# Retention then MLP: the first block's stores moved to ScalarE's queue, with a new order of loads and new planner numbers

## The chip, the cores and the metric

The kernel runs on one core of one Trainium2 chip. The metric is the time of one execution in device microseconds, lower is better. TensorE (PE in the profile) multiplies matrices, VectorE (DVE), ScalarE (ACT) and GpSimd (POOL) work on tiles, SyncE (SP) only issues DMAs here. 16 DMA engines move data for all of them.

## The reference, cut to what matters

```
B, H, S, D = 8, 8, 576, 64          # q, k, v: float32, B x H x S x D
scores = matmul(q, k^T) / sqrt(D)
gamma  = 1 - 2 ** (-5 - arange(H))
Dmat   = gamma[h] ** (i - j) if i >= j else 0
ret    = matmul(scores * Dmat, v)
x      = ret.transpose(0, 2, 1, 3).reshape(4608, 512)
h      = x @ w_in                   # 512 x 2048
g      = 0.5 * h * (1 + erf(h / sqrt(2)))
out    = g @ w_out                  # 2048 x 512, float32
```

## The kernel before

**Tiling.** The sequence of 576 is cut into four chunks of 128 and a tail of 64. A unit is one chunk of one batch (or the two tails of a pair of batches); 36 units of 128 tokens make nine blocks of 512 tokens. Units are taken in groups: groups 0 to 3 are the first chunks of the first four batches, one unit each (the "raw" units, in the tile `early`), and the groups from 4 on hold the same chunk of two batches. A group goes through these steps: its q and k are turned (groups 0 to 5 by TensorE, L454; the later ones by VectorE's 32x32 transposes, L548, with a copy that sorts them on ScalarE, L559), `scores` multiplies them into PSUM, `masked` multiplies by the mask on VectorE into `ret` (L612 for the raw units, L617 for the others), `inner` multiplies by v, `state` adds the chunk's keys times values to a running state, `cross` multiplies the state of the chunks before by q, and `evacuate` writes the result to the block's `x` tile.

**The two layers.** `mlp1` multiplies `x` by `w_in` and applies the Gelu on ScalarE (L816, L819) into `g_all`; `mlp2` multiplies by `w_out` into `o_sb`, which is stored. Block 0 is done in pieces of 128 or 256 tokens as its units and weights arrive. Later layers use a Strassen-like scheme with seven products in place of eight: `mlp2_fast` for the second half of block 0 and all later blocks, `mlp1_fast` for the last blocks. The products are named 1 to 7 and run in the order 1, 2, 6, 5, 7, 4, 3. They need sums of weights (`w_out_sums`, L870, eight instructions on VectorE, once all of `w_out` has landed) and of activations (`g_sum`, L883), intermediate copies `t` out of PSUM (`snap`, L485 on VectorE or L487 on ScalarE), and joins on VectorE into `o_sb` (L901). Product 7 of a half block needs the copy `t2` made after product 6.

**The order is written out by a planner.** The Python code that builds the kernel keeps planned times `T` for each engine and appends at each turn of the loop at L1303 what it thinks is ready next. On the chip nothing is reordered: each engine runs its own list in order and waits for semaphores. So a planner number (a landing, a duration, a threshold such as `LEAD`, `NEAR`, `AHEAD`, `JOIN`) acts only through the order that comes out. Where the planner sees a gap at the start it appends matmuls of zeros (`warm`, L1256).

**Loads.** All loads but those of unit 0 are issued by GpSimd (`load`, L305), in the order of the string `ORDER` (L376), then group by group (`reload`, L389). In it `wi5` is 256 columns of `w_in`, `wo2` 256 rows of `w_out`, `q7` the queries of unit 7, `n8` the keys of units 8 and 9 in a second layout, `io` and `dq2` computations of constants. `sw_dma` plans a landing: a time to issue, and a time to move in one queue.

**Stores.** `put` (L1247) appends the DMA of one finished `o_sb` to SyncE's list, or at the very end partly to ScalarE's. `STORE_AT` is the planner's earliest time for the stores of block 0; SyncE's list holds nothing but the first loads and the stores, so a store on it starts as soon as its `o_sb` is written. `share` is the planner's account of what a store takes from the loads. The pool of `o_sb` has four buffers (L114): q, k and v of unit 0 use the first three of them, block 0 writes four `o_sb`, and block 1's first `o_sb` comes into the buffer of block 0's first one.

Of the kernel before, what the change touches and what calls it, by code (L numbers as in the profile page):

```python
# [17 lines left out]
def kernel(  # L18
# [14 lines left out]
    nc = tc.nc  # L33
# [50 lines left out]
    N_XB = 4  # L84
    AHEAD = 35
    RATE = 0.4
    STORE_AT = 62.0
    CROWD = 66.0
    STATE10 = 28.0
    HOT = 8.0  # L90
    FETCH = 5.0
    ARRIVE = 5.4
    WARM_TO = 24.0
    JOIN = 1
    JOIN_SB = 0.0
    VISIT = 8
    LEAD = -3.0
    NEAR = 3.2
    SLACK, SB, PER_G, PER_B, TURN0 = 1.2, 2.0, 8.0, 20.0, 0.0
    FINE = 0.38  # L100
    FPOOL = 0.6
    N_V = 6
    N_WARM = 10
    MSK_AT = -58.0
    HK = N_DF // 2
# [16 lines left out]
    SEM = 0.12  # L122
    OVER = {"dve": 0.06}

# [97 lines left out]

    later = [(7.3, "act", 1.4, warm_gelu), (MSK_AT, "dve", 0.8, make_msk)]
    T["act"], T["dve"], T["pool"] = 2.6, 2.9, 1.25

# [15 lines left out]
    def sw_dma(issue, move):  # L241
        if len(flying) >= 8:
            T["pool"] = max(T["pool"], flying[-8])
        at = T["pool"]
        T["pool"] += issue
        sw[0] = max(sw[0] + move, at + ARRIVE + move - 0.9)
        flying.append(sw[0])
        return sw[0]
# [56 lines left out]
    def load(what, i):  # L305
# [3 lines left out]
        if what == "wi":  # L309
            nc.gpsimd.dma_start(w_in[:, :, i * 256:(i + 1) * 256],  # L310
                                moe_w_in[:, i * 256:(i + 1) * 256].rearrange("(c p) f -> p c f", p=128))
            land_in[i] = sw_dma(0.79, 1.35)
            return
# [10 lines left out]
        if what == "wo":  # L324
            nc.gpsimd.dma_start(w_out[:, 2 * i:2 * i + 2, :],
                                moe_w_out[i * 256:(i + 1) * 256, :].rearrange("(c p) f -> p c f", p=128))
            land_out[i] = sw_dma(0.75, 1.36) + 0.5
            return
# [4 lines left out]
        if what in "qk" and group_of[i] in BY_PE:  # L333
            dst = qk["qk".index(what)].rearrange("p (h e j d) -> p e h j d", h=HP, e=2, j=2)[:, :, :, j]
            for e in range(2):
                nc.gpsimd.dma_start(dst[:, e], {"q": q, "k": k}[what][2 * bp + j, HP * e:HP * e + HP, ci * C:ci * C + C, :].rearrange("h s d -> s h d"))  # L336
                land[what, i] = sw_dma(FPOOL, 0.48)
            return
# [12 lines left out]
        if what == "n":  # L351
            nc.gpsimd.dma_start(kn.rearrange("p j e h d -> p (j e h) d"),  # L352
                                k[2 * bp:2 * bp + 2, :, ci * C:ci * C + C, :].rearrange("b h s d -> s (b h) d"))
            land[what, i] = land[what, i + 1] = sw_dma(1.27, 1.8)
            return
        if what == "v" and i >= 4 and j is not None:
            nc.gpsimd.dma_start(v_ld.rearrange("p j h d -> p (j h) d"),  # L357
                                v[2 * bp:2 * bp + 2, :, ci * C:ci * C + C, :].rearrange("b h s d -> s (b h) d"))
            land[what, i] = land[what, i + 1] = sw_dma(1.27, 1.8)
            return  # L360
        src = {"q": q, "k": k, "v": v}[what]
        for jj in (j,) if j is not None else range(2):
            n = C if j is not None else TAIL
            if what == "v":
                dst = v_ld if i < 4 else v_ld[:, j] if j is not None else v_ld[n * jj:n * jj + n, 0]
            else:
                dst = qk["qk".index(what)] if i < 4 else qk["qk".index(what)][0:n, :, jj]
            nc.gpsimd.dma_start(dst, src[2 * bp + jj, :, ci * C:ci * C + n, :].rearrange("h s d -> s h d"))
            land[what, i] = sw_dma(0.88, 0.9) if j is not None else sw_dma(0.68, 0.5)

# [4 lines left out]
    cast_due["v", 0] = (loaded[0][1], first["first_v"])  # L375
    ORDER = ("wi4 io wo2 q2 q1 k1 k2 wi5 wi3 n4 v1 wi1 v2 wi0 wi2 k3 q3 v3 wi7 dq2 wi6 wo6 q4 wo4 q5 wo0 wo1 wo3 "  # L376
             "wo5 k5 wo7 q6 k4 k7 v4 q7 k6 q8 v6 q12 dq0 q9 v12 k9 k13 q10 n8 k11 k8 v8 dq3 k10 q11 v10 k12 n10 "
             "dq4 q13 n6 n12").split()

# [161 lines left out]
    def turn_dve(n, x):  # L541
# [6 lines left out]
        nc.vector.transpose(dst.rearrange("p (h b t) -> p h t b", h=HP, b=32), src)  # L548
        done = on("dve", 0.13 + m / 530, max(land["qk"[x], i] for i in groups[n])) + SEM
        if x == 0:  # L550
# [4 lines left out]
    def apart():  # L555
# [4 lines left out]
                       sg[n]["pairs"].rearrange("p h s -> p (h s)")[:, 0:2 * m].rearrange("p (n y) -> p y n", y=2))  # L560
        sg[n]["T"] = max(sg[n].get("T", 0.0), on("act", 0.15 + m / 580, ready) + SEM)

# [241 lines left out]
    def act_dur(n):  # L804
        return 0.12 + n * 0.00084

# [440 lines left out]
    def put():  # L1247
        ready, t, ts, o_sb, lo, hi = stores.pop(0)
        rows = rows_of(t, ts)
        for m, (row, p0, n) in enumerate(rows):  # L1250
            ending = t == N_BLK - 1 and all(x[-1] == "3" for x in waiting2 if x[1] == t)
            queue = nc.scalar if ending and (m if len(rows) > 1 else ts % 2 == 0) else nc.sync
            queue.dma_start(out[row:row + n, lo:hi], o_sb[p0:p0 + n, lo:hi])
        share(T["pe"], 0.75 * (hi - lo) / d_model)

# [193 lines left out]
```

## Time and profile before

| | us |
|---|---|
| median of 3 runs | 287.59 (287.58 to 287.60) |
| the profiled execution | 288.46 |
| its span | 286.7 |
| TensorE busy in the span | 277.8 (97%) |
| VectorE, ScalarE, GpSimd busy | 229.7, 176.7, 141.0 |
| matmuls of zeros | 24 |
| last product's end, then join, store and its landing | from 282.95 to the end of the span |

The span lies 1.8 us below the profiled execution's own time, and the profiled execution 0.9 us above the median of the runs. Times within the span are counted from its start. In the timeline rows the first column is the start, the second the time from the start to the end of the merged group, and what stands in brackets is the engine's idle time before it and who ended it. "DMA to landing" counts from the start of the issuing instruction.

### The profile page before, as it was taken

Reading aid. Unit: us, or ns where it says so; the run is one execution under the profiler, and the core shown is the slowest. Engines: PE = TensorE matmul, PEld = TensorE weight load, DVE = VectorE, ACT = ScalarE, POOL = GpSimd, SP = SyncE. Lnnn points to the kernel's source line nnn. Section 1 sums busy time; section 2 is a strip of 40 time slices with the busy share of each in tenths; the row PEclk is TensorE's granted clock in tenths of the full one; section 3 lists DMA queues with packets and bytes.
Section 4 is the critical chain, followed back from the end, with each engine's and each line's share of the span. In section 5 each row is a group of like instructions: output and inputs, shape, how many; then the busy total and the mean of one; then the engine's idle time right before and its main releaser. Section 6 shows DMA issues by size and latency. Waiting matters only on the chain.

```text
span 286.7 us, 9851 instructions
## 1 busy us (share of the span) xinstructions
PE 277.8 (97%) x4216; PEld 210.3 (73%) x4216; DVE 229.7 (80%) x387; ACT 176.7 (62%) x403; POOL 141.0 (49%) x213
## 2 busy tenths in 40 slices
PE   7889998999999999999999999999999999999994
PEld 2568766888864657756676676677888888888883
DVE  6754586767995699898978599969999999999861
ACT  7456425876888895688587766764555363655421
POOL 8976898799959977778665864000000000000000
PEclk9999999999999999999999999999999999999999
DMA  9999999999999999999999996302020201202014
GB/s 158 176 179 188 195 152 173 188 132 143 128 154 108 116 167 120 205 146 135 142 150 160 101 139 54 71 2 75 2 75 0 77 4 72 75 0 75 37 57 129
DMA packets 109276, 31.97 MB, mean 112 GB/s; under 512 B 85936, under 2 KB 104880, under 8 KB 109232
## 3 DMA queue, kind: packets, MB, share of 16 engines
q0 software_dynamic: 100528, 21.12, 83.8%
q1 hardware_dynamic: 6752, 9.37, 9.9%
q10 hardware_dynamic: 1952, 0.85, 1.3%
q8 instruction: 33, 0.54, 0.8%
q14 instruction: 11, 0.09, 0.1%
HBM read 42.99 MB, written 9.44 MB: 183 GB/s over the span
## 4 chain that ended last, share of the span: by engine, by line
PE 61%; DMA 22%; POOL 12%; issue 2%; ACT 1%; DVE 0%; POOLq 0%
PE psum L450 60%; DMA kn_ld<-in_k_dram 6%; DMA w_out<-in_moe_w_out_dram 6%; DMA q_ld<-in_q_dram 5%; POOL k_ld L346 3%; POOL q_ld L346 2%; DMA v_ld<-in_v_dram 2%; DMA early<-in_q_dram 2%; POOL v_ld L357 2%; DMA k_ld<-in_k_dram 1%; POOL dqT L320 1%; PE psum L454 1%; POOL kn_ld L352 1%; POOL w_in L310 1%; POOL k_ld L336 1%
## 5 line engine op out<-in xcount | busy, mean ns | idle before, releaser
L450 PE MATMUL psum<-x,w_in 128*128 128x256 bf16 (+2 forms) x792 | 117.8, 295 | 0.6 <-DMA w_in<-in_moe_w_in_dram 0.6
L450 PEld LDWEIGHTS <-w_in 128*128 128x128 bf16 x792 | 69.0, 98 | 29.1 <-DMA w_in<-in_moe_w_in_dram 1.2
L450 PEld LDWEIGHTS <-g_all 128*128 128x128 bf16 x576 | 55.5, 98 | 13.5 <-issue 0.3
L450 PE MATMUL psum<-w_out,g_all 128*128 128x256 bf16 (+1 forms) x440 | 57.9, 280 | 0.0
L346 POOL DMA_DIRECT2D k_ld<-in_k_dram x64 | 35.5, 577 | 23.8 <-DMA kn_ld<-in_k_dram 14.1
L816 ACT ACTIVATE g_all<-psum 128x512 bf16<-128x512 f32 x64 | 36.9, 592 | 16.4 <-PE psum L450 14.8
L450 PEld LDWEIGHTS <-s 128*128 128x128 bf16 x408 | 39.5, 98 | 7.6 <-issue 0.6
L634 ACT ACTIVATE vh<-v_ld,dv 128x128 bf16<-128x128 bf16 (+1 forms) x144 | 42.1, 378 | 0.0
L617 DVE TENSOR_TENSOR ret<-psum,msk 128x1024 bf16<-128x1024 f32 (+1 forms) x32 | 35.5, 1149 | 6.3 <-PE psum L450 6.2
L1030 ACT ACTIVATE g_all<-t 128x512 bf16<-128x512 f32 x36 | 22.6, 630 | 28.2 <-DVE t L1038 28.2
L487 ACT COPY t<-psum 128x256 f32<-128x256 f32 (+1 forms) x48 | 20.7, 433 | 29.7 <-PE psum L450 29.5
L346 POOL DMA_DIRECT2D q_ld<-in_q_dram x64 | 35.6, 583 | 1.9 <-DMA k_ld<-in_k_dram 1.0
L450 PE MATMUL psum<-wt,s 128*128 128x256 bf16 x272 | 33.5, 273 | 0.3 <-ACT t L487 0.3
L901 DVE TENSOR_TENSOR o_sb<-psum,t 128x256 f32<-128x256 f32 x51 | 21.4, 420 | 13.1 <-PE psum L450 7.2
L1038 DVE TENSOR_TENSOR t<-psum,t 128x512 f32<-128x512 f32 x36 | 24.6, 687 | 2.7 <-ACT t L487 1.1
L819 ACT ACTIVATE g_all<-psum 128x256 bf16<-128x256 f32 (+1 forms) x43 | 19.5, 488 | 11.2 <-PE psum L450 10.6
L485 DVE COPY t<-psum 128x512 f32<-128x512 f32 (+1 forms) x39 | 21.6, 564 | 0.4 <-PE psum L450 0.3
L450 PE MATMUL psum<-x,ws 128*128 128x256 bf16 x144 | 19.5, 273 | 0.0
L450 PE MATMUL psum<-wt,g_all 128*128 128x256 bf16 x136 | 17.5, 273 | 0.0
L450 PE MATMUL psum<-w_out,s 128*128 128x256 bf16 x136 | 17.5, 273 | 0.0
L357 POOL DMA_DIRECT2D v_ld<-in_v_dram x14 | 16.5, 1180 | 1.0 <-ACT g_all L816 0.7
L785 DVE TENSOR_TENSOR x<-psum,dqT 128x1024 bf16<-128x1024 f32 (+1 forms) x14 | 15.5, 1137 | 0.1
(100 smaller groups left out, 326.2 us busy)
## 6 DMA issues: line engine op xcount, KB each, us to landing
out_dram<-o_sb SPq DMA_DIRECT2D x31, 256.0 KB, 3.3
q_ld<-in_q_dram POOLq DMA_DIRECT2D x56, 64.0 KB, 5.5
k_ld<-in_k_dram POOLq DMA_DIRECT2D x56, 64.0 KB, 4.7
v_ld<-in_v_dram POOLq DMA_DIRECT2D x14, 256.0 KB, 5.3
kn_ld<-in_k_dram POOLq DMA_DIRECT2D x12, 256.0 KB, 6.8
w_in<-in_moe_w_in_dram POOLq DMA_DIRECT2D x8, 256.0 KB, 8.4
w_out<-in_moe_w_out_dram POOLq DMA_DIRECT2D x8, 256.0 KB, 7.1
q_ld<-in_q_dram POOLq DMA_DIRECT2D x16, 32.0 KB, 4.5
```

The source lines that it names most:

```text
L346: nc.gpsimd.dma_start(qk["qk".index(what)][p0:p0 + 32, 0:HP * per].rearrange("p (h x) -> p h x", h=HP), {"q": q, "k": k}[what][2 * bp + jj ...
L357: nc.gpsimd.dma_start(v_ld.rearrange("p j h d -> p (j h) d"), v[2 * bp:2 * bp + 2, :, ci * C:ci * C + C, :].rearrange("b h s d -> s (b h) d"))
L450: nc.tensor.matmul(*a, **k)
L485: nc.vector.tensor_copy(dst, src)
L487: nc.scalar.copy(dst, src)
L617: nc.vector.tensor_tensor(both.rearrange("p (e h) s -> p e h s", e=2), t, by, op=ALU.mult)
L634: nc.scalar.activation(vh[:, 0:m, h], src[:, :, h], AF.Copy, scale=dv[:, h, ci:ci + 1])
L816: nc.scalar.activation(g_all[:, t % 2, :, m0, :], hT.rearrange("p n (a c) -> p (n a) c", a=2), AF.Gelu)
L819: nc.scalar.activation(g_of(t, 2 * lo // TOK)[:, m0:m0 + n, lo_:lo_ + hi - lo], hT, AF.Gelu)
L901: nc.vector.tensor_tensor(dst, src, f[key], op=ALU.add)
L1030: nc.scalar.activation(g_of(t, part)[:, m0:m0 + 2], src, AF.Gelu)
L1038: nc.vector.tensor_tensor(f[key], f["b"][1], f[key], op=ALU.add)
```

## The change: what it does

The planner's numbers are changed, and `put`. Three things come out of it in the instruction lists. (1) The four stores of block 0 (256 KB each) leave SyncE's list and stand on ScalarE's, one behind the other, between the twelfth and the thirteenth Gelu of block 1. (2) GpSimd's list of loads has the same transfers in another order. (3) TensorE's list holds the same matmuls in another order, with 29 of zeros in place of 24; the attention steps come in the same number of visits (14 of scores for the full groups, five joint ones of two groups from `inner` on), except that the scores of the last two tails stand together. VectorE's mask instructions L213 and L215 move behind the first L612. Some copies out of PSUM change between VectorE and ScalarE, and four joint L785 become eight L789. The order of the last products is the same.

```diff
-    AHEAD = 35
-    RATE = 0.4
+    AHEAD = 18
+    RATE = 5.8
     STORE_AT = 62.0
-    CROWD = 66.0
-    STATE10 = 28.0
+    CROWD = 200.0
+    STATE10 = 12.0
...
-    JOIN = 1
+    JOIN = 0
     JOIN_SB = 0.0
     VISIT = 8
-    LEAD = -3.0
-    NEAR = 3.2
+    LEAD = -2.0
+    NEAR = 1.6
...
-    FINE = 0.38
-    FPOOL = 0.6
+    FINE = 0.35
+    FPOOL = 0.55
...
-    MSK_AT = -58.0
+    MSK_AT = 18.0
...
-    OVER = {"dve": 0.06}
+    OVER = {"dve": 0.08, "act": 0.09}
...
-    T["act"], T["dve"], T["pool"] = 2.6, 2.9, 1.25
+    T["act"], T["dve"], T["pool"] = 2.6, 2.9, 1.4
...
-        sw[0] = max(sw[0] + move, at + ARRIVE + move - 0.9)
+        sw[0] = max(sw[0] + move, at + (ARRIVE if at < 4.0 else 3.9) + move - 0.9)
...
-            land_in[i] = sw_dma(0.79, 1.35)
+            land_in[i] = sw_dma(0.78, 1.32)
...
-            land_out[i] = sw_dma(0.75, 1.36) + 0.5
+            land_out[i] = sw_dma(0.75, 1.28) + 0.3
...
-                land[what, i] = sw_dma(FPOOL, 0.48)
+                land[what, i] = sw_dma(0.74, 0.44)
...
-            land[what, i] = land[what, i + 1] = sw_dma(1.27, 1.8)
+            land[what, i] = land[what, i + 1] = sw_dma(1.17, 1.68)
...
-            land[what, i] = sw_dma(0.88, 0.9) if j is not None else sw_dma(0.68, 0.5)
+            land[what, i] = sw_dma(0.88, 0.9) if j is not None else sw_dma(0.7, 0.55)
...
-    ORDER = ("wi4 io wo2 q2 q1 k1 k2 wi5 wi3 n4 v1 wi1 v2 wi0 wi2 k3 q3 v3 wi7 dq2 wi6 wo6 q4 wo4 q5 wo0 wo1 wo3 "
-             "wo5 k5 wo7 q6 k4 k7 v4 q7 k6 q8 v6 q12 dq0 q9 v12 k9 k13 q10 n8 k11 k8 v8 dq3 k10 q11 v10 k12 n10 "
-             "dq4 q13 n6 n12").split()
+    ORDER = ("wi1 io wi7 k1 n4 v2 wi5 q1 q2 k2 wi0 dq2 v1 q3 wi4 v3 wi2 k3 wo2 wo7 wi6 k4 wi3 wo1 wo0 wo3 wo5 k5 "
+             "wo4 wo6 k6 q4 q5 v4 q8 v8 n8 q6 k9 q7 k7 v6 q10 n6 k8 q9 k11 k10 v12 q11 k13 v10 n10 dq3 n12 q12 k12 "
+             "dq0 q13 dq4").split()
...
-        done = on("dve", 0.13 + m / 530, max(land["qk"[x], i] for i in groups[n])) + SEM
+        done = on("dve", m / 457 - 0.02, max(land["qk"[x], i] for i in groups[n])) + SEM
...
-        sg[n]["T"] = max(sg[n].get("T", 0.0), on("act", 0.15 + m / 580, ready) + SEM)
+        sg[n]["T"] = max(sg[n].get("T", 0.0), on("act", 0.18 + m / 595, ready) + SEM)
...
-        return 0.12 + n * 0.00084
+        return 0.16 + n * 0.00084
...
-            queue = nc.scalar if ending and (m if len(rows) > 1 else ts % 2 == 0) else nc.sync
+            queue = nc.scalar if t == 0 or ending and (m if len(rows) > 1 else ts % 2 == 0) else nc.sync
+            if t == 0:
+                on("act", 0.6)
             queue.dma_start(out[row:row + n, lo:hi], o_sb[p0:p0 + n, lo:hi])
-        share(T["pe"], 0.75 * (hi - lo) / d_model)
+        share(T["pe"], 1.2 * (hi - lo) / d_model)
```

More of the change, by code (lines that the diff above doesn't have):

```diff
@@ L358, in load @@
                                 v[2 * bp:2 * bp + 2, :, ci * C:ci * C + C, :].rearrange("b h s d -> s (b h) d"))
-            land[what, i] = land[what, i + 1] = sw_dma(1.27, 1.8)
+            land[what, i] = land[what, i + 1] = sw_dma(1.17, 1.68)
             return
```

## The prediction

> **What bounds the kernel now.** I read the page first, then the busy times by stage, the waits of TensorE, the chain that ended last, and the timeline of each engine around the waits.
>
> ```profile
> span 286.7 us, 9851 instructions
> PE 277.8 (97%) x4216; PEld 210.3 (73%) x4216; DVE 229.7 (80%) x387; ACT 176.7 (62%) x403; POOL 141.0 (49%) x213
> PE   7889998999999999999999999999999999999994
> DMA  9999999999999999999999996302020201202014
> q0 software_dynamic: 100528, 21.12, 83.8%
> ```
> ```profile
> 9.00:16.00 7.00, 6.12 (x97) 3.95 (x97) 5.57 (x12) 1.88 (x5) 6.04 (x9) 1.00 1.92 177
> 16.00:33.00 17.00, 16.10 (x315) 14.43 (x311) 7.06 (x12) 10.44 (x26) 13.02 (x18) 1.00 1.67 187
> 33.00:41.00 8.00, 7.99 (x45) 3.95 (x43) 7.02 (x12) 1.61 (x4) 6.50 (x9) 1.00 1.73 156
> 41.00:51.03 10.03, 8.90 (x203) 7.19 (x201) 6.88 (x9) 5.18 (x14) 8.99 (x14) 1.00 1.60 167
> 51.03:283.00 231.97, 231.53 (x3537) 177.90 (x3536) 196.39 (x312) 150.69 (x343) 98.56 (x153) 1.00 0.82 98
> ```
>
> TensorE is busy for 97% at a granted clock of 1.00, and the same matmuls run after the change. So the time can move only by TensorE's idle time and by matmuls of zeros, which count as busy. In the 232 us after 51.03 it idles 0.44 us: there is next to nothing to win, and only something to lose. Before that it idles 0.88, 0.90 and 1.13 us in three stages, beside the zeros. The DMA digits stay at 9 until some 170 us: the loads' queue q0 is full, and at the start it sets what TensorE can do.
>
> ```profile
> PE psum L454 <- DMA q_ld<-in_q_dram: 1.1, 1, 1.1
> PE psum L450 <- DMA w_in<-in_moe_w_in_dram: 0.6, 1, 0.6
> PE psum L450 <- ACT t L487: 0.3, 1, 0.3
> 45.94 0.61 PE L454 MATMUL psum<-ident,q_ld 128*128 128x128 bf16 x8 [1.08 <-DMA q_ld<-in_q_dram]
> 39.69 6.11 DMA q_ld<-in_q_dram
> ```
> ```profile
> L1253 SPq DMA_DIRECT2D out_dram<-o_sb x2: 356/358/361, 40.5 to 41.0; - x2
> DMA to landing us min/median/max: 5.2/5.4/5.7
> L1253 SPq DMA_DIRECT2D out_dram<-o_sb x2: 332/332/332, 50.7 to 51.6; - x2
> DMA to landing us min/median/max: 5.7/6.0/6.3
> ```
>
> The longest wait after the first microseconds is for the queries of group 5. Their last DMA is issued at 39.7 and lands at 45.8, and in between SyncE starts the first two stores of block 0, at 40.5 and 41.0, because nothing holds its queue back. The other two start at 50.7 and 51.6.
>
> **Stores: what goes.** The first pair no longer collides with group 5's queries, so the 1.08 us at 45.94 goes, if nothing else is late at that place. What is late next there is the queue itself, in the new order. I rebuild it from four landings on the chain that ended last, each row's start plus its time.
>
> ```profile
> 4.14 6.38 DMA early<-in_q_dram
> 18.43 9.51 DMA w_out<-in_moe_w_out_dram
> 28.94 7.12 DMA w_out<-in_moe_w_out_dram
> ```
>
> That is q1 at 10.5, wo6 at 27.9 and wo5 at 36.1. Between the last two the queue landed five pieces of w_out and four of 64 KB in 8.1 us: 1.28 each and 0.43 each. Between the first two it landed eight weights and seven 128 KB transfers in 17.4 us; with 1.30 and 0.88 that is 16.6, so 0.8 us was lost underway.
>
> **Loads: the new order up to 51 us.** At 10.5 the new order has landed the same amount (wi1, wi7, k1, v2). From there wi5 comes at 11.8, q1 at 12.7, q2 at 13.6, k2 at 14.5, wi0 at 15.8, v1 at 16.7, q3 at 17.5, and k3 at 21.9, or 22.7 with the 0.8 lost. From k3 to the last w_out are ten weights and two pairs of 64 KB (14.5 us): 36.4 to 37.2. Then k6, q4 and q5, three pairs, end at 39.0 to 39.8.
>
> ```profile
> 7.58 1.47 PE L450 MATMUL psum<-zeros 128*128 128x512 bf16 x6
> 9.67 0.40 PE L450 MATMUL psum<-ret,early 128*32 128x128 bf16 x14 [0.36 <-DVE ret L612]
> 7.11 0.47 DVE L213 TENSOR_SCALAR msk<-val 128x128 f32<-128x128 f32 x1
> 8.32 1.29 DVE L612 TENSOR_TENSOR ret<-psum,near 128x512 bf16<-128x512 f32 x2
> 14.09 0.81 PE L450 MATMUL psum<-zeros 128*128 128x512 bf16 x3
> 28.98 2.41 PE L450 MATMUL psum<-x,w_in 128*128 128x128 bf16 x40
> 31.23 0.61 PE L454 MATMUL psum<-ident,q_ld 128*128 128x128 bf16 x8
> 33.01 8.12 PE L450 MATMUL psum<-w_out,g_all 128*128 128x512 bf16 x40
> 51.03 0.62 PE L450 MATMUL psum<-q_ld,kT 32*128 32x128 bf16 x32
> 51.59 3.67 PE L450 MATMUL psum<-x,w_in 128*128 128x256 bf16 x32
> 55.18 0.63 PE L450 MATMUL psum<-ret,vh 128*32 128x128 bf16 x32
> 56.35 7.16 PE L450 MATMUL psum<-x,w_in 128*128 128x256 bf16 x64
> ```
>
> Before, the masks from 7.11 to 8.32 stand ahead of the first L612; behind it, they let unit 0's second half start some 0.5 us sooner, at 9.1 where the zeros end. TensorE then has four zeros (0.22 each by the row at 14.09) and reaches its first w_in at 10.3. From there to 17.5 it follows the landings above, and the five zeros more (1.1 us) lie in these gaps: they cost nothing of their own, and if the loads came earlier they would cost up to 1.1. It turns q3 at 17.6 to 17.8. The work from there to k3's turn (inner of unit 2, a state, 64 matmuls with w_in) is 4.4 us at the paces of the rows (0.056 for 128 columns: 40 from 28.98 to 31.23), so TensorE is there at 22.2 and waits 0 to 0.5. The rest of block 0's first layer is 10.1 us more: it ends between 32.6 and 33.1. Before it ended at 33.01, with a turn of 0.44 (31.23 to 31.67) in it that now comes later: 32.6 for the same work. So the start is 0 to 0.5 us slower; I take 0.3, nearer to the later end, since 0.8 us was lost in the same stretch of the queue before.
>
> From 33.01 to 51.03 it was 18.0 us. Without the idle 1.08, and with the turn of 0.44 that has moved in, it is 17.4, so the point that stood at 51.03 comes at 50.0 to 50.5. The turn of group 4's queries is due 6.9 to 7.0 after the first layer's end, at 39.5 to 40.1, and finds them landed at 39.0 to 39.8: hardly any cover, so 0.5 us of delay in the queue costs up to 0.5. Group 5's queries come after three 256 KB loads (as four of 64 KB, 1.7 each) and four pairs, 8.5 us behind q5: 47.5 to 48.3, and they are due at 48 to 48.5. That cover is as thin. The eight L870 start when the last w_out lands, as before, and end ahead of the first scores. This part is worth 0.5 to 1.0 us; I take 0.7.
>
> **Stores: what comes.** ScalarE now issues them after the twelfth Gelu of block 1.
>
> ```profile
> L1253 ACTq DMA_DIRECT2D out_dram<-o_sb x4: 499/556/600, 281.3 to 283.4; - x4
> 53.45 1.56 ACT L819 ACTIVATE g_all<-psum 128x512 bf16<-128x512 f32 x3
> 51.10 2.44 ACT L634 ACTIVATE vh<-v_ld,dv 128x128 bf16<-128x128 bf16 x8
> 43.92 2.35 DVE L617 TENSOR_TENSOR ret<-psum,msk 128x1024 bf16<-128x1024 f32 x2 [0.96 <-PE psum L450]
> 42.54 0.42 DVE L901 TENSOR_TENSOR o_sb<-psum,t 128x256 f32<-128x256 f32 x1 [0.24 <-PE psum L450]
> 72.57 0.69 DVE L883 TENSOR_TENSOR s<-g_all 128x1024 bf16<-128x1024 bf16 x1
> ```
>
> Four issues of 0.56 are 2.2 us of ScalarE. Queued behind them are the last four Gelus of block 1, a cast of the state and the copies `t` of product 1; TensorE waits for these only when its PSUM banks run out. ScalarE is busy for 150.7 of 232 us in this stage, and its list there (cast, eight scaled values of 2.4, a sorting copy, Gelus of 0.5) puts the first issue at 64 to 65.5. I cost the issue itself at 0 for that slack, at most 0.5.
>
> The landing is the dearer part. From 50.3 on, TensorE's list has twice 48 matmuls with w_in (0.11 each), a scores visit (0.56) and an attention visit (1.2, 55.18 to 56.35), 64.5; then 24, scores to 67.8, 8 and the products 1 and 2: 70.5. The join of product 2, L901, writes into the buffer of block 0's first store. With a store's 5.2 to 6.3 us this buffer is free at 70 to 71.5. Behind the waiting L901 on VectorE stand an L883 (0.69) and the copy `t2` (as long as the join, 0.42), on which product 7 waits. Masks (2.35 after the scores at 67.8), join, sum and copy end at about 72.1, and product 7 is due at 72.3, two products after product 2. So a late landing passes to TensorE in full. I take 0, the ends are 0 and 1.
>
> **The rest.** The late loads have slack: their bytes and their order by groups are unchanged from group 9 on, and TensorE's only wait on another engine after 51.03 is the 0.3 for a copy `t`. I count 0.1 gained there, with bounds of -0.4 and +0.5, since the new lists put other work ahead of each copy. The four L785 split in two add some 0.1 each on VectorE, beside TensorE's work. The last products and joins are the same list: nothing.
>
> The sum is 0.7 + 0.1 = 0.8 us off the span, 285.9, and with the 1.8 us around it 287.7 for a profiled execution. That of before (288.46) lies 0.87 above the median of the runs, so 286.8.
>
> **A page on shared engines.** The Trainium skill, "DMA: Bandwidth & Descriptors", section "Issuing engines are not separate DMA queues", says that DMAs started by ScalarE, SyncE or GpSimd end up on the same 16 engines and interleave. The 6.11 us of group 5's queries beside SyncE's stores agree with it. By this page moving a store to another queue saves nothing by itself; only its new time can.
>
> **The rivals.** *The new place collides too, and VectorE pays* (slower). Four stores in a row at 65 on a full queue, 1 MB where pairs were sent before: if the first lands over 5.5 us after its issue, or is issued past 65.5, L901 waits, then the copy, then product 7. With twice the pair's traffic, 8 us to landing, the wait is some 2.3 us, 289.1, and a third of it gives 287.6. For it: the chain above has 0.2 us of slack. Against: the first store of a pair had 5.2 and 5.7, and the others stand behind it. I put it at 288.5, with 0.25.
>
> *The start eats the gain* (no change). The queue holds TensorE from 10 to 23 us; with the 0.8 us lost ahead of q3 instead of behind it, or with group 4's queries late by 0.5, the 0.7 us is gone: 287.6. The 29 zeros speak for it. 0.14.
>
> *The collision is only moved* (no change). The stores push the loads behind them by some 2.4 us (group 5's queries, a weight, a 256 KB load and five pairs after 36.1, would have landed at 43.4, not 45.8), and if a later group's turn then waits 1 us, as group 5's did, it is 287.6. Against it: the second pair at 50.7 pushed them too, and no wait on a DMA came after 51. 0.06.
>
> *All small waits go* (faster). The late 0.44 goes too, and the start does not lose its 0.3: 286.8 - 0.4 - 0.3 = 286.1. The landings at their earlier values speak for it, VectorE's 196 busy us of 232 after 51.03 against it. 0.12.
>
> **How the numbers follow.** About 0.2%, 0.58 us, is what can be told from no change. My forecast of 286.8 has 0.43; most of it (0.39) lies below 287.0. Faster: 0.39 + 0.12 = 0.51. Same: 0.04 + 0.14 + 0.05 = 0.23. Slower: 0.25 + 0.01 = 0.26. The range runs from 285.8, just past the faster rival, to 288.5, the middle of the slow one.
>
> **What would show it.** Right: no wait of TensorE on q_ld near 46, the first scores of group 5 0.5 to 1 us nearer to the start for the same work, four stores on ScalarE's queue at 64 to 65.5 with 5 to 6 us to landing, and less than 0.5 us of idle TensorE after that. Wrong: L901 near 70 idle on a DMA of o_sb and TensorE idle before product 7; a wait on early or q_ld at 17 to 23 or at 40; or new waits on `t` copies late in the span.

## The result, and the profile after

| | before | after |
|---|---|---|
| median of the runs, us | 287.60 (287.53 to 288.66, 6 runs) | 295.86 (295.27 to 296.40, 6 runs) |
| ratio | 1 | 1.028 [1.026, 1.030] |
| profiled execution, its span | 288.46, 286.7 | 296.32, 294.5 |

The change costs 2.8%, and the spans of the two profiled executions differ by 7.8 us. The page after:

```profile
span 294.5 us, 9865 instructions
PE 280.8 (95%) x4221; PEld 211.0 (72%) x4221; DVE 227.3 (77%) x386; ACT 179.0 (61%) x408; POOL 140.7 (48%) x213
PE   7889999999999999599999899999999999999995
DMA  9999999999999999999999991302010202100214
q0 software_dynamic: 100528, 21.12, 81.6%
```

TensorE is no longer full in the middle: one slice shows 5. The busy times by stage (length, then PE, PEld, DVE, ACT, POOL, then PEclk) say where, and the waits of TensorE behind 30 us say for whom:

```profile
51.28:64.50 13.22, 13.22 (x263) 11.05 (x264) 10.39 (x11) 11.35 (x28) 12.80 (x20) 1.00 1.66 143
73.90:119.00 45.10, 45.10 (x938) 29.80 (x936) 38.73 (x58) 34.27 (x87) 35.95 (x57) 1.00 1.22 123
119.00:129.00 10.00, 6.60 (x61) 3.72 (x60) 5.22 (x9) 6.07 (x15) 6.69 (x11) 0.83 1.55 155
155.00:167.00 12.00, 10.85 (x131) 7.06 (x130) 9.41 (x12) 9.68 (x25) 9.36 (x16) 1.00 1.62 145
124.80:128.20 3.40, 3.40 (x34) 1.84 (x34) 1.45 (x2) 1.92 (x5) 3.36 (x5) 0.50 1.05 85
```
```profile
PE psum L450 <- ACT u_acc L709: 3.4, 1, 3.4
PE psum L450 <- DVE t L485: 1.1, 1, 1.1
PE psum L450 <- DVE ret L617: 0.7, 2, 0.4
PE psum L454 <- DMA k_ld<-in_k_dram: 0.3, 1, 0.3
```

The wait on `q_ld` at 46 is gone. In its place TensorE idles 3.4 us before 123.6, then runs 3.4 us at a granted clock of 0.50, which by an estimate costs another 1.7 (half of the 3.4). Here are TensorE and then ScalarE at that place:

```profile
118.30 1.90 PE L450 MATMUL psum<-x,w_in 128*128 128x512 bf16 x8
123.60 1.03 PE L450 MATMUL psum<-w_out,g_all 128*128 128x256 bf16 x8 [3.40 <-ACT u_acc L709]
```
```profile
116.08 0.60 ACT L816 ACTIVATE g_all<-psum 128x512 bf16<-128x512 f32 x1
120.64 2.44 ACT L634 ACTIVATE vh<-v_ld,dv 128x128 bf16<-128x128 bf16 x8 [3.96 <-DMA v_ld<-in_v_dram]
122.99 1.04 ACT L709 COPY u_acc<-psum 128x512 f32<-128x512 f32 x2
```

The eight scaled values (`vh`) of group 14 stand on ScalarE's list ahead of the copies of the state (L709), and nothing overtakes them. Their load lands at 120.6. Until then PSUM is not emptied and TensorE stops. Before, the same L634 stood behind L709 and began 7 us after its load had landed (at 118.6 by the trace's DMA records, which hold the time of each landing). So the landing is 2.0 us later than before, and the place in the list is about 9 us earlier: ScalarE comes to it at 116.7. ScalarE of the kernel before:

```profile
120.63 1.18 ACT L709 COPY u_acc<-psum 128x512 f32<-128x512 f32 x2 [1.49 <-DVE u_sb L707]
125.51 2.43 ACT L634 ACTIVATE vh<-v_ld,dv 128x128 bf16<-128x128 bf16 x8
```

A smaller case of the same kind is on VectorE, before TensorE's wait of 1.14 us at 166.40. A turn (L548) that waits for group 19's queries stands ahead of the copies `t`:

```profile
161.51 1.10 DVE L548 STREAM_TRANSPOSE qT<-q_ld 128x512 f32<-128x512 f32 x1 [2.06 <-DMA q_ld<-in_q_dram]
165.05 1.05 DVE L548 STREAM_TRANSPOSE kT<-k_ld 128x512 f32<-128x512 f32 x1
165.96 0.39 DVE L485 COPY t<-psum 128x256 f32<-128x256 f32 x1
```

The start, which was forecast to end (first `w_out` product) at 32.6 to 33.1:

```profile
12.12 0.62 PE L450 MATMUL psum<-x,w_in 128*128 128x128 bf16 x8 [0.76 <-DMA w_in<-in_moe_w_in_dram]
20.03 3.26 PE L450 MATMUL psum<-x,w_in 128*128 128x256 bf16 x40 [0.75 <-DMA w_in<-in_moe_w_in_dram]
29.13 5.03 PE L450 MATMUL psum<-x,w_in 128*128 128x128 bf16 x72 [0.50 <-ACT x L487]
34.00 1.24 PE L450 MATMUL psum<-w_out,g_all 128*128 128x512 bf16 x5
```

And block 0's stores (the four of L1255 on ScalarE's queue between 60 and 75 us):

```profile
L1255 ACTq DMA_DIRECT2D out_dram<-o_sb x4: 367/669/1120, 64.6 to 66.4; - x4
DMA to landing us min/median/max: 6.3/6.7/7.0
```

**A ledger of the runs.** A sum of idle times can't be compared between lists of another order. So every matmul but those of zeros gets the mean spacing of its kind in the trace of before (from its start to the next one's, where TensorE did not idle), and the ledger reads off when each kernel had done the same amount of this work. The table shows how many us later than before that was, at seven of before's times, and the difference of the spans at the end. It is worked out from one profiled execution of each kernel, and is good to about half a microsecond; the ratio from the runs stands behind it. The ratios compare fast runs with fast runs, and e4_no_mid_stores has no row because its profiled execution was a slow one. The profiled execution of e2 was the longest of its four runs, those of e1, p2 and h1 were the shortest of theirs, so their ends differ from what the ratio says.

| kernel | 30 | 54 | 65 | 111 | 123 | 157 | 167 | end | ratio |
|---|---|---|---|---|---|---|---|---|---|
| after | 1.4 | 0.4 | 1.0 | 1.0 | 5.8 | 5.3 | 6.9 | 7.8 | 1.028 |
| e1_sync_stores | 1.3 | 2.8 | 3.7 | 3.7 | 3.6 | 3.1 | 3.2 | 3.9 | 1.020 |
| e2_v14_early | 1.4 | 0.7 | 1.2 | 2.7 | 2.5 | 4.5 | 8.1 | 9.9 | 1.030 |
| k1_no_first_stores | 1.6 | 0.8 | 1.2 | 1.1 | 1.0 | 0.6 | 2.5 | 3.4 | 1.012 |
| n1_turn19_early | 1.1 | 1.0 | 1.8 | 2.0 | 2.0 | 1.5 | 1.6 | 2.4 | 1.011 |
| m2_pair_50 | 1.0 | 0.6 | 3.4 | 3.6 | 4.1 | 4.0 | 6.1 | 7.1 | 1.024 |
| g3_after_oldland | 1.5 | 0.9 | 5.3 | 7.9 | 7.3 | 9.0 | 9.4 | 10.3 | 1.033 |
| m1_oldland_sync | 1.3 | 1.6 | 1.7 | 2.1 | 1.5 | 3.3 | 3.6 | 4.8 | 1.018 |
| g2_after_oldorder | 1.4 | 0.2 | 1.2 | 1.6 | 1.0 | 3.6 | 5.2 | 7.0 | 1.026 |
| g1_before_neworder | 1.2 | 2.0 | 2.2 | 7.5 | 7.0 | 7.3 | 7.3 | 11.8 | 1.042 |
| p1_before_newmodel | 0.3 | 4.0 | 4.1 | 6.4 | 7.4 | 17.5 | 17.6 | 20.1 | 1.069 |
| p2_before_newthr | 1.6 | 0.0 | 0.0 | 1.7 | 1.2 | 2.4 | 2.5 | 3.0 | 1.020 |
| e3_before_act | 0.2 | -1.3 | -1.3 | 1.1 | 1.1 | 0.9 | 0.9 | 0.8 | 1.005 |
| h1_pair_46 | -0.1 | -1.4 | -0.9 | -0.9 | -0.8 | -1.2 | -1.2 | -1.5 | 1.001 |
| h2_pair_49 | 0.1 | -0.7 | 0.3 | 0.3 | 0.3 | 0.0 | 0.0 | -0.2 | 1.002 |
| b1_before_no_first | 0.1 | -1.1 | -1.1 | -1.1 | -1.1 | -1.3 | -1.3 | -1.4 | 0.997 |

### The profile page after: what moved, and what is told of

The parts are those of the page before. It is cut to its first block, busy times and chain, and to the rows that moved or that the text cites. A ratio compares the mean times of both kernels' runs of the same rounds, so it can differ in the third digit from the quotient of the medians.

```text
span 294.5 us, 9865 instructions
## 1 busy us (share of the span) xinstructions
PE 280.8 (95%) x4221; PEld 211.0 (72%) x4221; DVE 227.3 (77%) x386; ACT 179.0 (61%) x408; POOL 140.7 (48%) x213
## 5 line engine op out<-in xcount | busy, mean ns | idle before, releaser
L450 PE MATMUL psum<-x,w_in 128*128 128x256 bf16 (+2 forms) x792 | 119.8, 296 | 2.4 <-DMA w_in<-in_moe_w_in_dram 1.5
L450 PEld LDWEIGHTS <-g_all 128*128 128x128 bf16 x576 | 55.9, 98 | 20.1 <-issue 6.3
L450 PE MATMUL psum<-w_out,g_all 128*128 128x256 bf16 (+1 forms) x440 | 59.2, 283 | 3.6 <-ACT u_acc L709 3.4
L634 ACT ACTIVATE vh<-v_ld,dv 128x128 bf16<-128x128 bf16 (+1 forms) x144 | 42.0, 379 | 4.0 <-DMA v_ld<-in_v_dram 4.0
L819 ACT ACTIVATE g_all<-psum 128x256 bf16<-128x256 f32 (+1 forms) x43 | 20.0, 488 | 10.8 <-PE psum L450 10.1
L548 DVE STREAM_TRANSPOSE qT<-q_ld 128x512 f32<-128x512 f32 (+1 forms) x16 | 15.0, 939 | 8.0 <-DMA q_ld<-in_q_dram 8.0
L450 PE MATMUL psum<-wt,g_all 128*128 128x256 bf16 x136 | 17.5, 273 | 1.1 <-DVE t L485 1.1
L883 DVE TENSOR_TENSOR s<-g_all 128x1024 bf16<-128x1024 bf16 x17 | 12.3, 726 | 7.7 <-ACT g_all L819 6.6
L548 DVE STREAM_TRANSPOSE kT<-k_ld 128x512 f32<-128x512 f32 (+1 forms) x16 | 15.0, 939 | 3.5 <-DMA k_ld<-in_k_dram 3.5
```

The source lines that it names most:

```text
L450: nc.tensor.matmul(*a, **k)
L634: nc.scalar.activation(vh[:, 0:m, h], src[:, :, h], AF.Copy, scale=dv[:, h, ci:ci + 1])
L819: nc.scalar.activation(g_of(t, 2 * lo // TOK)[:, m0:m0 + n, lo_:lo_ + hi - lo], hT, AF.Gelu)
```

## The experiments

### What the place of the stores costs

**The stores back on SyncE, in the changed kernel** (e1_sync_stores):

```diff
-            queue = nc.scalar if t == 0 or ending and (m if len(rows) > 1 else ts % 2 == 0) else nc.sync
+            queue = nc.scalar if ending and (m if len(rows) > 1 else ts % 2 == 0) else nc.sync
```

> The changed kernel with the four stores of block 0 back on SyncE's list; every other list is the same. Theory A (ScalarE's list puts the scaled values of group 14, which wait for their v, ahead of the copies that free a PSUM bank): the stores have little to do with it; the wait of 3.4 us at 120 stays within 0.7, and the time stays within 1.0 us of 295.9. Theory B (the stores at 65 to 73 push the load stream back, and so the v of group 14): the stores go out at some 42 to 53 us, the wait at 120 shrinks by 2 us or more together with the half clock behind it, and the time falls by 3 us or more. Beside either: with stores at 42 to 53 the turns of group 5 collide again and cost up to 1 us.

Measured 1.0198 [1.0153, 1.0243]. The collision is back, and larger:

```profile
51.78 0.61 PE L454 MATMUL psum<-ident,q_ld 128*128 128x128 bf16 x8 [2.79 <-DMA q_ld<-in_q_dram]
```

but the stop at 120 and the half clock are gone, with the same list of ScalarE and the same bytes to store. Group 14's values land at 118.7 (DMA records), just before the list asks for them:

```profile
119.29 2.45 ACT L634 ACTIVATE vh<-v_ld,dv 128x128 bf16<-128x128 bf16 x8
```

So in the new lists the late place of the stores is the dearer one, by some 2.4 us after the ratios, although it removes the wait that it was meant for. Theory B is right about the stop; the time falls by less than the 3 us that it gave.

**Block 0's stores cut to one row of 64 numbers each, in the changed kernel** (k1_no_first_stores):

```diff
+            if t == 0:
+                queue.dma_start(out[row:row + 1, lo:lo + 64], o_sb[p0:p0 + 1, lo:lo + 64])
+                continue
             queue.dma_start(out[row:row + n, lo:hi], o_sb[p0:p0 + n, lo:hi])
```

> The changed kernel with its four stores of block 0 cut to one row of 64 numbers each (the rest of these rows isn't written), still issued by ScalarE at 64 to 66. Theory S (the late stores push the loads of groups 12 to 16 by some 2 us, and ScalarE's list passes that on at 120): the values of group 14 land at 118 to 119 and not at 120.6, the 3.4 us of idle TensorE and the half clock behind it are gone, ratio 1.008 to 1.016. Rival (the loads are late for other reasons): the wait at 120 stays over 2 us, ratio 1.022 or more.

Measured 1.0123 [1.0059, 1.0187]. The values of group 14 land at 116.0 (DMA records), 4.6 us sooner than in the changed kernel, and ScalarE, with the same list, does not wait:

```profile
116.74 2.44 ACT L634 ACTIVATE vh<-v_ld,dv 128x128 bf16<-128x128 bf16 x8
119.52 1.18 ACT L709 COPY u_acc<-psum 128x512 f32<-128x512 f32 x2 [0.34 <-DVE u_sb L707]
```

This is the strongest pair: the stores, where the changed kernel has them, make 4.4 of the 7.8 us (7.8 less 3.4 in the ledger; 4.5 by the ratios, with an interval of some 2.6 to 6.4), by pushing the loads behind them. The other 3.4 us are there without them. The pair prices the stores against none, not against their old place: that comparison is e1, which ends 3.9 us earlier in the ledger and 2.4 us by the ratios.

**The stores of blocks 1 and 2 cut instead** (e4_no_mid_stores; the same edit with `t in (1, 2)`):

> The changed kernel with the stores of blocks 1 and 2 cut to one row of 64 numbers each (so these rows of the output stay unwritten); the lists are the same otherwise. Theory D (the stores of blocks 1 and 2, eight of 256 KB from 77 on, fall in the stretch where the loads of groups 12 to 14 move, and set how late the v of group 14 is): it lands by 116 to 118 in place of 120.6, and the wait of 3.4 us falls below 1 us without the half clock behind it, 291 to 292. Theory A alone, with these stores of no weight: it lands within 0.7 us of 120.6 and the time stays within 1 us of 295.9.

Measured 1.0132 [1.0077, 1.0188]. In its profiled execution group 14's values land at 117.9, and the stop at 120 is gone. So taking bytes away elsewhere ahead of that load helps too; it need not be block 0's. But the number of bytes does not decide alone: e1 stores them all, from 41.2 on, and has no stop either.

**The same move in the kernel before** (e3_before_act; only `t == 0 or` is added to the choice of the queue, so that the lists of TensorE and VectorE stay):

> The kernel before with this one edit: the four stores of block 0 on ScalarE's list, where its planner puts them (behind the eleventh Gelu or so of block 1); all other lists are the same. Theory A and the prediction's first step: TensorE's wait of 1.1 us for q_ld at 46 goes and nothing comes for it, 286.5 (286.2 to 287.0). Theory B: the stores near 62 push the loads, the wait of 0.3 us at 123 grows by 1 to 3 us, and the time is 288 or more.

Measured 1.0054 [1.0028, 1.0080], slower although the 1.08 us at 46 goes (ledger: -1.3 at 54). ScalarE's issue, which the prediction cost at nothing, is paid at 66, on ScalarE and then on TensorE:

```profile
65.53 2.44 ACT L634 ACTIVATE vh<-v_ld,dv 128x128 bf16<-128x128 bf16 x8 [2.66 <-issue]
66.32 2.16 PE L450 MATMUL psum<-ret,vh 128*32 128x128 bf16 x32
```

Here `issue` is the four DMA starts, which run on ScalarE's sequencer from 62.28 to 65.49. The 32 matmuls take 2.16 and not 0.63 us, since they follow the scaled values one by one. TensorE has another wait of 0.47 us at 74.5, for which the profile shows no cause.

**One pair moved by a few us, in the kernel before** (h1_pair_46, h2_pair_49): a copy of the two DMA starts in `fire`, at planned 45 or 46, and `put` leaves them out.

```diff
+        for ready, t, ts, o_sb, lo, hi in stores if now >= 45.0 else ():
+            if t == 0 and ts < 2 and ts not in sent and ready <= now:
+                sent.add(ts)
+                for row, p0, n in rows_of(t, ts):
+                    nc.scalar.dma_start(out[row:row + n, lo:hi], o_sb[p0:p0 + n, lo:hi])
```

> The kernel before, with only the first two stores of block 0 moved: off SyncE, where they start at 40.5 and 41.0, to ScalarE's list behind the eight scaled values that end at 46.1; everything else, the other pair on SyncE at 50.7 and 51.6 too, is the same. Theory 1 (a store costs what it pushes away): at 46.1 the queries of group 5 have landed (43.4 to 44 without the stores), so the wait of 1.08 us at 45.94 goes, and the landings behind 50 are late by as much as before; the two issues of 0.56 hold back one copy t by up to 0.8. Gain 0.3 to 1.1 us: ratio 0.996 to 0.999. Rival (the queue is full until some 170 us, so half a megabyte costs its 2.5 us wherever it goes): another wait of about 1 us on a load between 47 and 60, ratio 0.999 to 1.003. Slower than 1.003 would say that ScalarE's issue itself is dear.

> As the one with the pair at 46, but with the pair one step further down ScalarE's list, behind the copy of kT that ends at 49.1, so that it goes at 49 to 50, right ahead of SyncE's second pair at 50.7: four stores in 2.5 us. If a burst of four is what costs (theory 2: four at 62 to 64 made the kernel before 0.5% slower), this one is slower than the one with the pair at 46 by 0.5 to 1.5 us, and group 7 or the values of group 6 land 2 us later than before. If only the collision with group 5's queries counts, both give the same, 0.996 to 0.999.

Measured 1.0007 [0.9989, 1.0025] and 1.0021 [1.0004, 1.0037]. The profiled execution of the first has no wait on `q_ld` behind 30 us and is 1.5 us shorter, the median isn't. That of the second still waits 0.43 us for `q_ld`; its pair went at 47.2 and 47.6. In the first the stores also went sooner than I had placed them, at 43.87 and 44.27, in the middle of the scaled values that they follow in the list (ACTq is ScalarE's sequencer):

```profile
43.51 0.69 ACT L634 ACTIVATE vh<-v_ld,dv 128x128 bf16<-128x128 bf16 x2
43.87 0.37 ACTq L1250 DMA_DIRECT2D out_dram<-o_sb  x1
44.10 0.39 ACT L634 ACTIVATE vh<-v_ld,dv 128x128 bf16<-128x128 bf16 x1
44.27 0.44 ACTq L1250 DMA_DIRECT2D out_dram<-o_sb  x1
44.40 1.56 ACT L634 ACTIVATE vh<-v_ld,dv 128x128 bf16<-128x128 bf16 x5
```

**The bound: block 0's stores cut to one row each in the kernel before** (b1_before_no_first, the edit of k1):

> The kernel before with its four stores of block 0 cut to one row of 64 numbers each, still on SyncE at 40 to 52 (the rest of these rows isn't written): the most that any other place for them could win in this list. If the collision with group 5's queries is all they cost, the wait of 1.08 us goes and nothing else: ratio 0.995 to 0.998. If the time of this list is not set by that wait (a pair moved to 46 left the median where it was), 0.998 to 1.001.

Measured 0.9966 [0.9951, 0.9981]: 1.0 us is all that any place for these stores could have won in the lists of before. It is the wait of 1.08, read rightly; no place that I tried brought it in.

**One pair at 49, in the changed kernel** (m2_pair_50: the edit of h1 at planned 48, the other pair on SyncE):

> The changed kernel with block 0's first two stores on ScalarE at 50 to 51, after group 5's queries have landed at 48.9, and the other two on SyncE at 50 to 54, ten us sooner than in the changed kernel; all else as changed. If the collision at 48 (2.8 us with the stores on SyncE at 41) and the late burst at 65 are both avoided, what is left is the start (1.3 us) and small waits: ratio 1.005 to 1.012. If the new lists lose the rest wherever the stores go, 1.015 or more.

Measured 1.024 [1.0174, 1.0306], not the hoped 1.005 to 1.012. The four stores now start between 48.9 and 52.1, as a burst at another place. A wait of 1.02 us for `q_ld` at 49.77 is left of the collision, the late burst is gone, and the load of other values lands later (55.8, 53.1 in the changed kernel), which ScalarE's list again passes on:

```profile
55.83 2.44 ACT L634 ACTIVATE vh<-v_ld,dv 128x128 bf16<-128x128 bf16 x8 [1.76 <-DMA v_ld<-in_v_dram]
59.77 0.42 PE L450 MATMUL psum<-vh,k_ld 128*32 128x64 bf16 x32 [0.99 <-ACT g_all L819]
```

### What removing one wait is worth

**The values of group 14 from an earlier load** (e2_v14_early):

```diff
+        if n == 14:
+            src = loaded[groups[12][0]][1][:, 0:m]
```

> The changed kernel, but the scaled values of group 14 are made from the v of group 12, which landed long before; all lists are the same, and only the wait for the landing goes (so the output of group 14 is that of other values). Theory A: TensorE's wait of 3.4 us at 120 and the 3.4 us at half clock behind it go, 5.1 us together, 290.8. Theory C (the whole load stream is late for this order, and the next load takes the place of this one): the wait of VectorE for the queries of group 15 and the other landings come through to TensorE, and less than half of the 5.1 us returns, 293.4 or more.

Measured 1.030 [1.0256, 1.0344]. The stop at 120 goes (2.5 at 123 in the ledger, not 5.8). But TensorE waits 1.68 us at 131.8 for a turn, and 3.6 us are lost between 157 and 167, where the changed kernel lost 1.6. This is theory C: the wait alone was not the cause; the loads behind are as late.

**The turn of group 19 from an earlier load, without the first stores** (n1_turn19_early; k1 and `loaded[groups[18 if n == 19 else n][0]]` in `turn_dve`):

> The changed kernel with its first stores cut to one row (1.012 in the run before) and, besides, the turn of group 19 made from group 18's queries and keys, which have long landed: VectorE's list is the same, but its L548 near 157 no longer waits 2.65 us for a load. If the idle 1.13 us of TensorE at 162 and the slow stretch behind it come from this turn standing ahead of the copy t in VectorE's list, 2 to 2.8 us go: ratio 1.002 to 1.006. If the loads behind are late as well, the next wait takes its place and the ratio stays at 1.010 or more.

Measured 1.0111 [1.0076, 1.0146], within the interval of k1. The loss between 157 and 167 falls from 1.9 to 0.1 in the ledger, as intended, and the span is 1.0 us shorter than k1's. The ratios do not resolve it, and the 1.002 to 1.006 that was expected if this turn made the loss did not come.

### Which other part makes the lists bad

**The new order of loads alone** (g1_before_neworder: the new string `ORDER` in the kernel before), and **the landings of before in the changed kernel** (g3_after_oldland: 1.80 for the 256 KB loads, 0.38 and 0.48 for the small ones, `ARRIVE` everywhere):

> The kernel before with the new order of loads and nothing else changed: its stores on SyncE, its planner's durations and thresholds as before (five more matmuls of zeros at the start come with the order). If the loss comes from the planner's new landings (steps listed ahead of their data) and from the late stores, this one costs only its start and a collision of its own: ratio 1.000 to 1.008, no wait of over 1 us behind 100 us. If the new order of loads is itself what makes groups 12 to 19 late, 1.012 to 1.025 with waits on t, kT or u_acc between 105 and 190.

> The changed kernel with the landings of before in its planner (the 256 KB loads 1.80 and not 1.68, the small ones 0.38 and 0.48, 5.4 us and not 3.9 from issue to landing); its order of loads, thresholds and late stores stay. The attention of groups 12 to 15 then stands later in TensorE's list. If the planner's early landings make the loss (theory 1), the idle 3.4 us at 120 and the half clock behind it go and the ratio falls from 1.028 to 1.008 to 1.016, what is left being the start and the stores. If the late stores alone make it, the ratio stays at 1.022 or more, since the stores go where they went.

Measured 1.0423 [1.0391, 1.0456] and 1.0330 [1.0298, 1.0362]: both worse than the whole change, and the first above what either theory gave. In it, TensorE stops in the middle of a visit, probably for its own instructions (the last section has the evidence), then has a mean clock of 0.79 over eight us (the second row is that stretch):

```profile
107.64 0.24 PE L450 MATMUL psum<-vh,kn_ld 128*32 128x64 bf16 x8 [2.84 <-issue]
104.00:112.00 8.00, 4.75 (x117) 3.26 (x113) 6.22 (x10) 5.40 (x22) 5.74 (x9) 0.79 1.43 140
```

In the second, VectorE's join of product 2 waits for block 0's late store to free its buffer, and TensorE behind it. This is the first link of my first rival's chain, in a neighbour of the changed kernel:

```profile
68.00 0.42 DVE L901 TENSOR_TENSOR o_sb<-psum,t 128x256 f32<-128x256 f32 x1 [5.07 <-DMA out_dram<-o_sb]
68.48 3.85 PE L450 MATMUL psum<-x,w_in 128*128 128x256 bf16 x20 [3.55 <-DVE o_sb L901]
```

**The same with the stores on SyncE** (m1_oldland_sync: g3 with the edit of e1):

> The changed kernel with the planner's landings of before (as in the run before, 1.033, where a join waited 5.07 us at 68 for a store of block 0) and block 0's stores back on SyncE. If that run lost its 4.9 us between 54 and 65 to the late stores' buffers, they go, a collision of 1 to 3 us at 48 comes in their place, and the ratio falls to 1.012 to 1.022. If the lists themselves are at fault, 1.028 or more.

Measured 1.0184 [1.0146, 1.0221], as expected: 4.1 us less than g3, and 3.6 us less by 65 in the ledger.

**The old order of loads in the changed kernel** (g2_after_oldorder):

> The changed kernel with the order of loads of before; its planner, thresholds and late stores on ScalarE stay. Theory A (the new order of loads costs 1.2 to 1.8 us at the start, and what comes behind is the late stores and lists ahead of their data): the end of block 0's first layer goes back to 33.0 to 33.3, and behind 51 this kernel still loses 2 to 6 us, ratio 1.008 to 1.020. Theory B (the order of loads makes nearly all of the loss, as it did when the kernel before got it alone, 1.042): ratio 0.998 to 1.006, no idle time of TensorE over 1 us behind 51.

Measured 1.0261 [1.0203, 1.0319], above what either theory gave. The stop is not at 120 but at 134: ScalarE's sorting copy waits for VectorE's turn, and a Gelu behind it holds TensorE. The turn had itself waited 3.90 us for its queries.

```profile
133.03 1.04 ACT L559 COPY q_ld<-qT 128x1024 bf16<-128x1024 bf16 x1 [2.76 <-DVE qT L548]
134.62 1.91 PE L450 MATMUL psum<-w_out,g_all 128*128 128x256 bf16 x16 [2.44 <-ACT g_all L816]
```

The start stays 1.4 us late with the old order of loads, so its loss does not need the new one. But g1, with the new order and the old thresholds, is 1.2 us late at 30 too and ends the first layer at 33.71: the new order makes such a loss by itself.

**The new landings and durations alone, and the new thresholds alone, in the kernel before** (p1_before_newmodel, p2_before_newthr; the lines of the diff above that are neither `ORDER` nor the queue, split between the two):

> The kernel before with only the planner's new landings and durations (loads, casts, turns, vector copies, the share of a store); order of loads, thresholds and stores as before. Theory: each part that makes the planner write another list loses on its own, since the list of before fits its landings as a whole; this one puts the scores of groups 15 to 19 up to 17 us (160 to 143) sooner in TensorE's list than their loads land, so 1.010 to 1.030 with waits on kT, t or vh between 100 and 170, and no loss at the start (its masks stay early). Rival: durations nearer to the traced ones alone make a better list, 0.995 to 1.003, and the loss sits in the thresholds and the order of loads.

> The kernel before with only the new thresholds (masks at 18 us in place of the first microseconds, a state's cast at 12 and not 28, joins, lead, how near two visits may stand); order of loads, landings, durations and stores as before. If the thresholds make the start's loss (first unit's halves closer, four zeros more), block 0's first layer ends 0.8 to 1.4 us later than 33.0, and with the new list behind it 1.008 to 1.030. If the start is not theirs, it ends at 32.8 to 33.2, and the order of loads and the landings are each what costs there.

Measured 1.0686 [1.0648, 1.0724] and 1.0196 [1.0142, 1.0250]. The first is far above the 1.010 to 1.030 that was expected: the landings alone make the worst list of all. VectorE's turn waits 4.65 us for group 18's queries, the masks stand behind it, and TensorE behind them:

```profile
150.59 1.08 DVE L548 STREAM_TRANSPOSE qT<-q_ld 128x512 f32<-128x512 f32 x1 [4.65 <-DMA q_ld<-in_q_dram]
151.52 2.33 DVE L617 TENSOR_TENSOR ret<-psum,msk 128x1024 bf16<-128x1024 f32 x2
```
```profile
152.78 0.21 PE L450 MATMUL psum<-q_ld,kT 32*128 32x128 bf16 x1 [3.63 <-DVE ret L617]
```

The thresholds alone show the start's loss, with the old loads and the old landings:

```profile
30.57 1.95 PE L450 MATMUL psum<-x,w_in 128*128 128x128 bf16 x32 [0.93 <-ACT x L487]
34.59 1.67 PE L450 MATMUL psum<-w_out,g_all 128*128 128x512 bf16 x7
```

That is 1.6 us behind before's 33.01, where the landings alone end this layer at 33.50.

## Why the prediction was wrong, by its own steps

**What bounds the kernel: right.** Behind 51 us there was only something to lose, and nearly all was lost there: in the ledger the changed kernel is 0.4 late at 54 and 7.8 at the end.

**Stores, what goes: right, and its size too.** The wait on `q_ld` went. b1 puts its whole worth at 0.34% [0.19, 0.49], 1.0 us.

**Loads, the new order up to 51: the start was mis-sized.** I took 0.3 us, bounds 0 to 0.5; the ledger has 1.4 at 30, and the point that stood at 51.03 came at 51.28, not at 50.0 to 50.5. (The sum also has a gap: 22.2 to 22.7 and 10.1 make 32.3 to 32.8, not 32.6 to 33.1.) From the end of the first layer to that point it took 17.28 us, where I had 17.4. The mistake was to work the start out from the queue of loads alone: p2 has a loss of this size without the new loads, and g2 keeps it with the old ones. The thresholds' order of the first units (masks later, other zeros, 0.50 us of waiting for ScalarE's `x`), which I had counted as a gain of half a microsecond, costs by itself. So do the new loads: g1 has 1.2 without the thresholds. The two do not add up, and how the 1.4 us divide between them stays open.

**Stores, what comes: right in place, wrong in price.** They were issued at 64.6 to 66.4, where I had 64 to 65.5, and took 6.3 to 7.0 us. The join and product 7 did not wait for them, so the rival on VectorE did not decide (in g3 it did). But the cost was not 0 to 1 us: 4.4 by k1, and 3.9 of it (2.4 by the ratios) against the old place, by e1. So this term of the sum failed: I priced the issue and the buffer, and left out the loads behind 1 MB of stores, on DMA engines that are full until some 170 us. The rival "the collision is only moved" said this, at 2.4 us of push, a wait of 1 us and a chance of 0.06. The push at group 14 was 4.6 us against no stores, 1.9 against e1 and 2.0 against the kernel before, and the wait was 3.4 with 1.7 of half clock behind it.

**The rest: this step failed.** I counted 0.1 gained, bounds -0.4 and +0.5; k1, without the stores, loses 2.6 us from 54 to the end. I had counted so because bytes and order of the late loads were unchanged and only one wait of 0.3 showed after 51. But slack is not a property of a load. It is the distance between its landing and the place where a list asks for it: group 14's values had 7 us in the list of before, and in the new one the list asked 3.9 us ahead of the landing. The landing moved by 2.0 us, the list's place by the rest. The lists were all replanned, and I read their groups, not the load each in-order engine comes to next.

What the four parts do alone is shown: stores 1.005, thresholds 1.020, order of loads 1.042, landings and durations 1.069. They don't add up to the 1.028 of the whole. Every kernel of these runs whose lists were planned anew lost about 1% or more, each new set of lists at another place. Most of the large stops (in the changed kernel, g2, g3, m2, p1) have one mechanism: a step that waits for a load or a store stands ahead of a step that TensorE needs, on an engine that runs in order. That the list of before is good because its numbers were fitted together is my reading, and argued only. Up to 64.5 TensorE does not idle (13.22 of 13.22); of the 0.6 us that the changed kernel loses by 65, 0.39 is a wait for `ret` right behind, at 65.25. The 0.9 us after 167 lie in small waits, and no run isolates them.

**Another queue won nothing.** The Trainium skill, "DMA: Bandwidth & Descriptors", section "Issuing engines are not separate DMA queues", says that DMAs from different engines interleave on the same 16. The pair on ScalarE's queue (1.0007) and all four (1.0054) agree with it: neither is faster. Both moved the stores in time as well, so no run here shows the queue alone.

## What to carry to other kernels

When a change rewrites instruction lists, find for each in-order engine the steps that wait for a load and what stands behind them, and compare the list's place with the traced landing: that distance is the slack, and a quiet trace of the old list says nothing of the new one's. A store moved off a collision is priced by its bytes too: here, on full DMA engines, four stores of 256 KB made a load 50 us later land 4.6 us later than without them. Before working for a wait's removal, cut the transfer that causes it out altogether: that run bounds the gain (here 1.0 us) for the cost of one experiment.

## What the runs showed of the hardware

- A DMA start in ScalarE's list did not wait for the engine to finish the work ahead of it: in h1 it came at 43.87, while the eight instructions ahead of it in the list ran until 45.96.
- Four DMA starts in a row on ScalarE held back the compute behind them: in e3 the engine stood idle for 2.66 us until the last of them was over at 65.49.
- TensorE's granted clock fell to 0.50 for 3.41 us after idle times of 2.84 (g1), 3.40 (after), 3.55 (g3) and 3.63 us (p1), some 1 us after TensorE had resumed. It stayed at 1.00 after 2.79 (e1) and 2.44 (g2). But in p1 it also fell, at 48.01, after waits of only 2.17 and 0.52 us with 0.61 us of work between them. So the length of one idle time does not decide alone.
- TensorE probably ran out of instructions in g1: the packets of what is likely its instruction queue (33 of 16 KB) came at 91.8 and then at 105.1, elsewhere in that stretch some 4 to 8 us apart, and it stood for 2.84 us until 107.64 in the middle of 32 equal matmuls, with no releaser in the profile. That the full DMA queues held the packet back is a guess that no run tests.
